# The last 64 tokens of v: from GpSimd's queue to SyncE's, and the first weights one per unit

## The chip, the cores and the metric

The kernel runs on one core of one Trainium2 chip. Five engines work side by side, each with its own queue of instructions in order: TensorE (PE; its weight loads are PEld), VectorE (DVE), ScalarE (ACT), GpSimd (POOL) and SyncE (SP). SP computes nothing and issues transfers. Sixteen transfer engines move data between memory and the core. The metric is the time of one execution on the device in microseconds, as the median of several runs; lower is better.

## The reference

There are two stages. The first is attention over a window of 128 tokens with a bias by distance, for 8 batches, 8 heads, 576 tokens and 64 numbers per head. The second takes attention's output as x (8 batches, 576 tokens, 512 channels), transforms it along the tokens, multiplies each of the 64 lowest modes by a complex matrix of its own, transforms back and mixes channels.

```
scores = q @ k.T / sqrt(64) - slope[h] * (i - j)      where 0 <= i - j < 128, else -1e9
x      = softmax(scores) @ v                          # heads side by side: (8, 576, 512)
X      = rfft(x over tokens)
Y[m]   = X[m] @ (w_r[m] + 1j * w_i[m])                for the modes m < 64, else 0
u      = x + irfft(Y)
out    = u + max(u @ w_ch, 0)
```

The two weights w_r and w_i hold 64 x 512 x 512 numbers each, 134 MB together, out of 164 MB that the kernel reads.

## The kernel before, in words

**Units and slots.** A unit is one pair of heads `s` of one batch `b`: 32 units (`g.units`, L69). The order comes from `GROUPS = ((0,), (1, 2, 3))` (L19): units 0 to 7 are pair 0 of the batches 0 to 7, and then come pairs 1, 2, 3 of batch 0, of batch 1, and so on. Attention runs in slots (`_slot`, L589), one for each unit, software-pipelined: in slot n come the scores of unit n (`_score`), the transposes of q and k of unit n+1 (`_tr`, evacuated by ACT in `_evac`), POOL's casts to bf16 of q and k of unit n+2 (`_cast_qk`) and of v of unit n+1 (`_cast_v`), and the product with v of unit n-1 (`_av`). The transposes take the PSUM buffers tagged `tqk`, of which there are two. The order of instructions on each engine is the order in which the program writes them; each engine waits at its next instruction until its inputs are there.

**Modes.** Pair 0's channels (rows 0 to 127 of each weight matrix) are multiplied between the slots from slot 10 on, two modes at a time (`_pair_of_modes`, `_modes`); the other 384 rows follow when attention is done. Weights come into a ring of 12,288 float32 per partition (`g.ring`). A part is two modes of w_r or of w_i: 512 KB for pair 0's rows, 1,536 KB for the other rows. The ring holds twelve of the small parts or four of the large. `_load_w` (L645) issues the next part if its place is free and does nothing if not; after each product with a part, `_modes` calls it as long as it succeeds. The steps from 16 modes on of the last group, the inverse transform and the mixing fill the rest of the time beside the weights, and `_finish` (L848) writes the output behind the last part.

**Transfers on SP's queue.** Loads ahead of the first slot are written in one loop (L126 to 134) over the units 0 to 15: q and k of the unit (`_load_unit`, one transfer each of 128 rows of 2,304 bytes, 288 KB), v of a unit (`_load_v`, two transfers of 128 KB in rows of 512 bytes; only the first 512 tokens), and from unit 7 on two calls of `_load_w`. As the ring has room for twelve small parts, the calls of units 7 to 12 take effect. v runs behind: v of unit n for n up to 4, and v of unit n-3 from unit 8 on. There are buffers for nine units of q and k (`QK`) and six of v (`VB`), so later loads wait for POOL's casts to free one. From slot 8 on each slot issues one more unit.

**The last 64 tokens of v.** The 576 tokens are four blocks of 128 and one of 64. v of the last 64 tokens has a tile of its own, `g.vbt`, in bf16: token p of the head `hh` of pair `s` on partition 64 `hh` + p, for each pair and batch, with a column of ones. `_load_vt` (L378) loads one pair `s` for all 8 batches: two transfers on POOL's queue, 128 KB each, in rows of 256 bytes (one token of one head). `_cast_vt` (L388) casts the pair with one POOL instruction of 128x512. Pair 0's load stands between the casts of units 0 and 1, ahead of the first slot, and its cast right behind the cast of v of unit 0 (L138 to 143). Pairs 1 to 3 are loaded in slots 2, 3 and 4 and cast in slots 4, 5 and 6 (L613 to 619). The one reader is the last pair of products in `_av` (L499), for every unit.

Of the kernel before, what the change touches and what calls it, by code (L numbers as in the profile page):

```python
# [9 lines left out]
FP32 = mybir.dt.float32  # L10
BF16 = mybir.dt.bfloat16
# [5 lines left out]
P = 128  # L17
MB = 8
GROUPS = ((0,), (1, 2, 3))  # L19
LA = 8  # L20
RING = 12288
JOINT = (2, 2)
ROWS = (2, 6)
VB = 6
# [12 lines left out]
LAST = (0, 3, 5, 6)  # L37

# [6 lines left out]
def kernel(  # L45
# [10 lines left out]
    nc = tc.nc  # L56
    B, H, S, D = q.shape
    NM, DM, _ = moe_w_r.shape
# [3 lines left out]
    g = Ctx()  # L62
# [27 lines left out]
    for b in range(B):  # L90
        t = [(g.x_sb[:, b, st], ((b, st * P), (b, st * P + 64))) for st in range(4)]
        if b % 2:
            t.append((g.x4[:, b // 2], ((b - 1, 4 * P), (b, 4 * P))))
        if b == B - 1:
            t = [t[4], t[1], t[0], t[3], t[2]]
        g.seq += t

    with tc.manual_schedule(engines={ET.SP, ET.PE, ET.Activation, ET.DVE, ET.Pool}):
        with ExitStack() as wctx:
# [5 lines left out]
            with ExitStack() as actx:  # L105
                cp = actx.enter_context(tc.tile_pool(name="const", bufs=1))
# [9 lines left out]
                g.vts = actx.enter_context(tc.tile_pool(name="vts", bufs=2))  # L116
# [9 lines left out]
                for n in range(n0):  # L126
                    _load_unit(g, n)
                    if n < VB - 1:
                        _load_v(g, n)
                    elif n >= VB + 2:  # L130
                        _load_v(g, n - 3)
                    if n >= g.first[1] - 1:
                        for _ in range(4 // JOINT[0]):
                            _load_w(g)
                with tc.tile_pool(name="tmpc", bufs=1, side="right") as tp:
                    _consts(g, tp)
                    _cast_qk(g, 0)
                    for s in GROUPS[0]:  # L138
                        _load_vt(g, s)
                    _cast_qk(g, 1)  # L140
                    _cast_v(g, 0)
                    for s in GROUPS[0]:
                        _cast_vt(g, s)
# [99 lines left out]
def _consts(g, tp):  # L243
# [15 lines left out]
    nc.gpsimd.memset(g.vbt[:, :, :, g.D : g.D + 1], 1.0)  # L259

# [117 lines left out]
def _load_vt(g, s):  # L378

    vt = g.vts.tile([P, g.B, g.D], FP32, tag="vt", name=f"vt{s}")  # L380
    for hh in range(2):
        g.nc.gpsimd.dma_start(
            out=vt[64 * hh : 64 * hh + 64],
            in_=g.v[:, 2 * s + hh, 512:576, :].rearrange("b p d -> p b d"))
    g.unit["vt", s] = vt


def _cast_vt(g, s):  # L388
    g.nc.gpsimd.tensor_copy(g.vbt[:, s, :, 0 : g.D], g.unit.pop(("vt", s)))
# [199 lines left out]
def _slot(g, n, w0, w1):  # L589
# [3 lines left out]
    if n == g.first[1] + 2:  # L593
        _select(g, 0, 0)
    if n < N:
        _score(g, n, 0)
# [16 lines left out]
    for j, grp in enumerate(GROUPS[1:]):  # L613
        for i, s in enumerate(grp):
            if n == g.first[j + 1] - 4 + i:
                _cast_vt(g, s)
        for i, s in enumerate(grp):
            if n == g.first[j + 1] - 6 + i:
                _load_vt(g, s)
# [300 lines left out]
```

## Time and profile before

| what | value |
|---|---|
| median of 3 runs | 449.3 us (448.2 to 451.52) |
| profiled execution, its own time | 450.29 us |
| its span | 448.5 us |
| busy PE / DVE / ACT / POOL | 294.1 / 216.1 / 189.6 / 139.1 us |
| bytes moved, mean rate | 173.86 MB, 388 GB/s |
| mean PE clock granted | 0.769 |
| POOL, casts of v (L409) | 128 of 64x256, 505 ns each |
| POOL, casts of q and k (L397) | 64 of 128x576, 768 and 859 ns each |
| POOL, issue of the tails (L382) | 8, 704 ns each, landing 7.5 us later (median) |
| POOL, casts of the tails (L389) | 4 of 128x512, 644 ns each; a wait of 4.5 us before the first |
| weights of pair 0's rows, issue to landing | 7.4 and 8.0 us (median of 32 and 33) |
| weights of the other rows, issue to landing | 13.8 and 13.7 us |

The span runs from the first to the last instruction of the profiled execution; the time holds a little more around it. A busy share is an average over stages with different limits: up to about 166 us there is attention with pair 0's modes between, up to 414 us the products with the other weights, and then the end. In the lists, L382 is line 382 of the kernel, `vt<-in_v_dram` means that the tile vt is written from the input v, and x8 that there were eight such instructions. In the chain of waits each line gives the start, the length and what the kernel waited for.

### The profile page before, as it was taken

To read this page: it belongs to the slowest core of one execution; us is meant where nothing else is said; L and a number is where in the kernel's file an instruction comes from. 1 tells how busy PE (TensorE), PEld (TensorE's weight loads), DVE (VectorE), ACT (ScalarE), POOL (GpSimd) and SP (SyncE) were. 2 spreads that over 40 slices of the span, in tenths; PEclk is the share of its full clock that TensorE was granted. 3 is DMA by queue.
4 is the path that set the end of the run, shared out by engine and by line. 5 is a ranking of instruction groups with operands and counts; after the bars stand their busy time and mean duration, and the time that the engine had idled before them with its cause. 6 is when DMAs were issued, how large, how long until landed. Compare 5 with 4: busy or idle time off the path is not lost.

```text
span 448.5 us, 12893 instructions
## 1 busy us (share of the span) xinstructions
PE 294.1 (66%) x5506; PEld 204.2 (46%) x5527; DVE 216.1 (48%) x427; ACT 189.6 (42%) x302; POOL 139.1 (31%) x257
## 2 busy tenths in 40 slices
PE   2467989887787885222235664854856748696993
PEld 2455767666666763111123333432433334464661
DVE  8458566566765661010002543453535345462882
ACT  3787656584866741000011331322313233251794
POOL 7699889586876702020000000000000000000700
PEclk9969576686988975555555988589778587899997
DMA  8999999999999999999999999999999999996498
GB/s 249 346 335 327 388 325 353 347 390 379 392 368 375 393 415 429 432 425 426 430 427 433 426 429 429 427 430 426 430 429 430 426 429 430 427 428 282 185 374 288
DMA packets 51562, 173.86 MB, mean 388 GB/s; under 512 B 4912, under 2 KB 21296, under 8 KB 43440
## 3 DMA queue, kind: packets, MB, share of 16 engines
q1 hardware_dynamic: 51120, 171.99, 97.2%
q0 software_dynamic: 384, 1.05, 0.9%
q8 instruction: 43, 0.70, 0.6%
q14 instruction: 15, 0.12, 0.1%
HBM read 163.58 MB, written 9.44 MB: 386 GB/s over the span
## 4 chain that ended last, share of the span: by engine, by line
DMA 50%; PE 26%; ACT 10%; DVE 6%; issue 4%; POOL 2%; ACTq 0%; POOLq 0%
DMA ring<-in_moe_w_r_dram 47%; ACT att L459 6%; PE acc L704 5%; PE sc L447 4%; PE xt L539 4%; PE u L825 3%; PE av L493 3%; DMA ring<-in_moe_w_i_dram 3%; ACT qkT L428 3%; PE tqk L420 2%; PE u L745 2%; POOL qkb L397 1%; PE xw L758 1%; DVE x_sb L507 1%; ACT mask L311 1%
## 5 line engine op out<-in xcount | busy, mean ns | idle before, releaser
L704 PE MATMUL acc<-Xz,ring 128*128 128x32 bf16 x2048 | 70.7, 183 | 100.2 <-DMA ring<-in_moe_w_r_dram 51.0
L704 PEld LDWEIGHTS <-ring 128*128 128x128 bf16 x2048 | 61.3, 101 | 130.1 <-DMA ring<-in_moe_w_r_dram 65.1
L763 ACT CAST hl<-xw 64x512 bf16<-64x512 f32 x72 | 41.7, 579 | 105.6 <-PE xw L758 70.9
L459 ACT ACTIVATE att<-sc 128x1024 bf16<-128x1024 f32 x64 | 65.6, 1025 | 32.8 <-PE sc L447 26.7
L764 DVE TENSOR_TENSOR hl<-xw,hl 64x512 bf16<-64x512 f32 x72 | 49.6, 688 | 58.1 <-ACT hl L763 57.8
L409 POOL CAST vb<-v 64x256 bf16<-64x256 f32 x128 | 64.7, 505 | 20.1 <-PE av L493 13.7
L783 POOL MEMSET ZTa<- 32x512 bf16 x2 | 1.0, 515 | 187.5 <-ACT ZTa L781 187.5
L447 PE MATMUL sc<-qkT,qkT 64*64 64x256 bf16 (+1 forms) x512 | 32.4, 330 | 30.1 <-ACT qkT L428 16.3
L758 PE MATMUL xw<-wch,xT 128*128 128x512 bf16 x138 | 46.3, 467 | 2.7 <-issue 2.2
L428 ACT COPY qkT<-tqk 128x576 bf16<-128x576 bf16 x64 | 40.7, 638 | 0.6 <-PE tqk L420 0.6
L420 PE MATMUL tqk<-ident_b,qkb 64*64 64x64 bf16 x1152 | 31.7, 214 | 7.6 <-POOL qkb L397 6.9
L420 PEld LDWEIGHTS <-qkb 64*64 64x64 bf16 x1152 | 30.8, 130 | 10.2 <-POOL qkb L397 9.2
L464 DVE TENSOR_TENSOR att<-att,mask 128x1024 bf16<-128x1024 bf16 x32 | 26.9, 839 | 14.7 <-ACT att L459 14.5
L585 ACT ACTIVATE Xz<-xz 128x192 bf16<-128x192 f32 (+1 forms) x24 | 7.5, 313 | 59.0 <-DVE Xz L584 57.9
L493 PE MATMUL av<-vb,att 128*128 128x65 bf16 (+1 forms) x512 | 30.8, 215 | 0.6 <-issue 0.2
L584 DVE CAST Xz<-xz 128x384 bf16<-128x384 f32 (+1 forms) x24 | 12.0, 511 | 36.4 <-PE xz L578 35.7
L447 PEld LDWEIGHTS <-qkT 64*64 64x64 bf16 x512 | 13.1, 120 | 35.3 <-ACT qkT L428 18.8
L397 POOL CAST qkb<-k 128x576 bf16<-128x576 f32 x32 | 27.5, 859 | 0.0
L493 PEld LDWEIGHTS <-att 128*128 128x128 bf16 (+1 forms) x512 | 24.4, 111 | 6.5 <-issue 0.6
L397 POOL CAST qkb<-q 128x576 bf16<-128x576 f32 x32 | 24.6, 768 | 6.1 <-PE tqk L420 3.3
L738 DVE COPY xT<-tp 128x512 bf16<-128x512 bf16 x36 | 15.2, 421 | 21.9 <-PE tp L736 21.4
L469 DVE TENSOR_TENSOR att<-att,mask 128x1024 bf16<-128x1024 bf16 x32 | 25.0, 780 | 1.5 <-ACT att L459 1.1
(104 smaller groups left out, 395.2 us busy)
## 6 DMA issues: line engine op xcount, KB each, us to landing
ring<-in_moe_w_r_dram SPq DMA_DIRECT2D x32, 1536.0 KB, 13.8
ring<-in_moe_w_i_dram SPq DMA_DIRECT2D x31, 1536.0 KB, 13.7
ring<-in_moe_w_i_dram SPq DMA_DIRECT2D x33, 512.0 KB, 8.0
ring<-in_moe_w_r_dram SPq DMA_DIRECT2D x32, 512.0 KB, 7.4
q<-in_q_dram SPq DMA_DIRECT2D x32, 288.0 KB, 6.3
k<-in_k_dram SPq DMA_DIRECT2D x32, 288.0 KB, 6.2
v<-in_v_dram SPq DMA_DIRECT2D x64, 128.0 KB, 5.8
out_dram<-o SPq DMA_DIRECT2D x32, 256.0 KB, 3.3
```

The costliest lines, as they stand in the source:

```text
L397: g.nc.gpsimd.tensor_copy(tb, t)
L409: g.nc.gpsimd.tensor_copy(o[64 * r : 64 * r + 64, i], v[64 * i : 64 * i + 64, r])
L420: g.nc.tensor.transpose(tp[hs, r, :], u.b[w][hs, r], g.ident_b[hs, hs], tile_position=(64 * hh, 64 * hh))
L428: g.nc.scalar.copy(dst.rearrange("c (p r) -> c p r", r=g.R), u.tp[w].rearrange("c r p -> c p r"))
L447: nc.tensor.matmul(sc[64 * r : 64 * r + 64, hh, 256 * i : 256 * i + nq], lhsT=kT[hs, c * P + r : c * P + P : 2], rhs=qT[hs, c * P : c * P ...
L459: nc.scalar.activation(a, sc, AF.Exp, scale=1.0 / math.sqrt(g.D))
L464: nc.vector.tensor_tensor(out=a, in0=a, in1=m, op=ALU.mult)
L493: nc.tensor.matmul(av[o, hh, col(t)], lhsT=att[c // 2][:, hh, q0 : q0 + m], rhs=u.vb[:, 2 * c + hh, 0 : D + 1], start=(j == 0), stop=(t < ...
L704: nc.tensor.matmul(acc[:, et, :, m0 - c0 : m0 - c0 + n, :], lhsT=wt[:, a, et * P : (et + 1) * P], rhs=X[:, a, 1 - w : 3 - w, m0 % MB : m0 ...
L758: nc.tensor.matmul(xw, lhsT=xT[:, dt], rhs=g.wch[:, dt], start=(dt == 0 and n in RELU), stop=(dt == 3))
L763: nc.scalar.copy(g.hl[own, n, h], xw[own])
L764: nc.vector.tensor_tensor(out=g.hl[other, n, h], in0=xw[own], in1=g.hl[own, n, h], op=ALU.subtract)
```

## The change

The tails of v are loaded by batch in place of by pair, on SP's queue in place of POOL's, and in rows of 512 bytes (two neighbouring tokens of one head) in place of 256. One batch is two transfers of 64 KB, each with four heads: 32 rows per head, laid on partitions as they come, so that partition 4p + h holds the tokens 2p and 2p+1 of head h of the four. Batch i of 0 to 7 is issued with unit 4, 5, 6, 7, 9, 10, 11 and 12 (`VT`), behind that unit's q, k and v. From unit 4 on each unit calls `_load_w` once, so that the twelve parts are spread over the units 4 to 15.

POOL casts a batch's tails as they lie, in one instruction of 128x256, first thing in slot b+1. Then PE puts the tokens on their partitions: four products with matrices of zeros and ones (`g.selv`, made at the start by POOL with one memset and four copies of the identity), 128x128 each with 128 columns, into a PSUM tile that shares the tag `tqk` with the transposes. DVE copies the result, 128x256, into `g.vbt`. The products stand behind slot b+1's scores and casts and ahead of the spectrum and `_av`. The tiles for the loaded tails have six buffers in place of two. The column of ones and everything that reads `g.vbt` are as before.

```diff
+VT = (4, 5, 6, 7, 9, 10, 11, 12)
...
-                g.vts = actx.enter_context(tc.tile_pool(name="vts", bufs=2))
+                g.vts = actx.enter_context(tc.tile_pool(name="vts", bufs=VB))
+                g.selv = cp.tile([P, 2, 2, P], BF16, name="selv")
...
-                    if n >= g.first[1] - 1:
-                        for _ in range(4 // JOINT[0]):
-                            _load_w(g)
+                    if n in VT:
+                        _load_vt(g, VT.index(n))
+                    if n >= VT[0]:
+                        _load_w(g)
...
-                    for s in GROUPS[0]:
-                        _load_vt(g, s)
                     _cast_qk(g, 1)
                     _cast_v(g, 0)
-                    for s in GROUPS[0]:
-                        _cast_vt(g, s)
...
+    nc.gpsimd.memset(g.selv, 0.0)
+    src = g.ident_b.rearrange("p (m i h) -> p i h m", i=2, h=2)
+    for r in range(2):
+        for i in range(2):
+            nc.gpsimd.tensor_copy(
+                g.selv[:, i, r].rearrange("p (h m r) -> p r h m", h=2, r=2)[:, r], src[:, i])
...
-def _load_vt(g, s):
-    vt = g.vts.tile([P, g.B, g.D], FP32, tag="vt", name=f"vt{s}")
-    for hh in range(2):
-        g.nc.gpsimd.dma_start(
-            out=vt[64 * hh : 64 * hh + 64],
-            in_=g.v[:, 2 * s + hh, 512:576, :].rearrange("b p d -> p b d"))
-    g.unit["vt", s] = vt
-def _cast_vt(g, s):
-    g.nc.gpsimd.tensor_copy(g.vbt[:, s, :, 0 : g.D], g.unit.pop(("vt", s)))
+def _load_vt(g, b):
+    vt = g.vts.tile([P, 2, 2, g.D], FP32, tag="vt", name=f"vt{b}")
+    for i in range(2):
+        g.nc.sync.dma_start(
+            out=vt[:, i].rearrange("p r d -> p (r d)"),
+            in_=g.v[b, 4 * i : 4 * i + 4, 512:576].rearrange("h (p r) d -> p h (r d)", r=2))
+    g.unit["vt", b] = vt
+def _cast_vt(g, b):
+    t = g.work.tile([P, 2, 2, g.D], BF16, tag="vtb", name="vtb")
+    g.nc.gpsimd.tensor_copy(t, g.unit["vt", b])
+    g.unit["vt", b] = t
+def _put_vt(g, b):
+    t = g.unit.pop(("vt", b))
+    ps = g.ps1.tile([P, 2, 2, g.D], FP32, tag="tqk", name="pvt")
+    for i in range(2):
+        for r in range(2):
+            g.nc.tensor.matmul(
+                ps[:, :, i], lhsT=g.selv[:, i, r], rhs=t[:, :, r], start=(r == 0), stop=(r == 1))
+    g.nc.vector.tensor_copy(
+        g.vbt[:, :, b, 0 : g.D], ps.rearrange("p j i d -> p (j i) d"))
...
+    if 0 <= n - 1 < g.B:
+        _cast_vt(g, n - 1)
     if n < N:
         _score(g, n, 0)
...
-    for j, grp in enumerate(GROUPS[1:]):
-        for i, s in enumerate(grp):
-            if n == g.first[j + 1] - 4 + i:
-                _cast_vt(g, s)
-        for i, s in enumerate(grp):
-            if n == g.first[j + 1] - 6 + i:
-                _load_vt(g, s)
+    if 0 <= n - 1 < g.B:
+        _put_vt(g, n - 1)
     if 0 <= n - 2 < N - 1:
         _spectrum(g, n - 2)
     if 0 <= n - 1 < N:
         _av(g, n - 1)
```

## The prediction

> **What bounds the kernel now.** I read the chain of waits first, then the page's transfer rows, then the stretches of time around the loads that the change moves, and last the waits of the engines that it touches.
>
> The chain of waits is made of compute alone up to 166 us and of weight transfers after that:
>
> ```profile
> 164.23 0.70 DVE att L469
> 164.98 0.82 PE av L493 x9
> 166.35 11.95 DMA ring<-in_moe_w_r_dram
> 178.35 0.84 PE acc L704 x24
> 179.20 13.68 DMA ring<-in_moe_w_r_dram
> ```
>
> From that alone, attention's compute would seem to bound the first 166 us. The transfer rows say that it does not bound alone:
>
> ```profile
> DMA  8999999999999999999999999999999999996498
> GB/s 249 346 335 327 388 325 353 347 390 379 392 368 375 393 415 429 432 425 426 430 427 433 426 429 429 427 430 426 430 429 430 426 429 430 427 428 282 185 374 288
> ...
> q0 software_dynamic: 384, 1.05, 0.9%
> ```
>
> The transfer engines are busy in every slice until the weights end, and only the bytes per second differ. So whatever takes transfer time early pushes the whole queue of weights, whose last part arrives at 414.17 us (issued at 401.60, 12.57 us in the chain); the stretch behind it is the same work. A smaller transfer bill is worth its own size at the end, as long as compute frees the buffers in time. The ring of weights shows that it does: SP issues part 12 at 67.16 us, though PE had used part 0, whose place it takes, by 58.9 us: 8 us in hand. Only from about 160 us does SP issue within a microsecond of PE's release, and there eight parts of 512 KB, about 10 us of transfer, are in flight.
>
> What do the tails of v (row q0, 1.05 MB, issued by POOL at L382) cost in that bill? These stretches show it (columns: stretch, its length, POOL busy, PE clock, share of the transfer engines, GB/s):
>
> ```profile
> core 0: us, POOL busy (x), PEclk, DMA share, GB/s
> 10.00:13.00 3.00, 0.01 (x1) 1.00 1.10 224
> 18.00:20.00 2.00, 1.89 (x4) 1.00 1.05 391
> 20.00:30.00 10.00, 9.59 (x17) 0.83 1.03 389
> 30.00:33.00 3.00, 2.87 (x6) 0.50 1.07 203
> 36.00:38.00 2.00, 1.64 (x4) 1.00 1.03 240
> 42.00:44.00 2.00, 1.94 (x4) 0.93 0.99 245
> 56.00:60.00 4.00, 2.54 (x5) 1.00 1.05 348
> 60.00:66.00 6.00, 5.70 (x11) 0.57 0.96 305
> 84.00:88.00 4.00, 0.49 (x1) 0.50 0.93 292
> 152.00:165.00 13.00, 3.32 (x6) 0.93 1.03 416
> ```
>
> Four times the engines are as busy as ever and move a little over half as much: 10 to 13, 30 to 33, 36 to 38 and 42 to 44 us. Each follows a pair of POOL's issues (5.56, 26.25, 30.99, 36.98 us), which land 7.5 us later.
>
> **The change, part by part, and its sum.** The sum is against the profiled execution, 450.29 us (span 448.5 and 1.8 around it). The median of the runs shown is 449.3, 1.0 lower; I take the difference found here off that median.
>
> *Old tails go.* The four stretches last 10 us and move 224x3 + 203x3 + 240x2 + 245x2 = 2,251 KB. With the 1,049 KB of tails taken out, 1,202 KB of other loads remain, which at 370 GB/s (between 348 and 389 in the rows beside them) need 3.2 us. The tails cost 10 - 3.2 = 6.8 us. Lower end: the packets' own time, 0.9% of 448.5 = 4.0 us. Upper end 7.5: some tail packets fall just outside the stretches. I take 6.8, since the loss of rate is seen directly.
>
> *New tails come.* 16 transfers of 64 KB in 512-byte rows. The nearest row is v itself, also 512-byte rows on SP's queue. Units without weights (590 KB of q and k, 262 KB of v) go at 348 GB/s in 56 to 60 us: 2.45 us each. The q and k alone go at 391 (18 to 20 us): 1.51 us. That leaves 0.94 us for 262 KB, so 3.8 us for all tails. By the 305 GB/s of 60 to 66 us it is 5.1 us. I take 4.2, nearer the first, because in 60 to 66 us the engines' share itself drops under 1. Transfer sum: -6.8 + 4.2 = -2.6; ends -7.5 + 3.8 = -3.7 and -4.0 + 5.1 = +1.1. The Trainium skill (DMA: Bandwidth & Descriptors, Specifications) says that rows reach line rate from 512 bytes on, and shorter ones are read and written back; at the 416 GB/s of the 4 KB rows the new tails would cost 2.5 us and the sum would be -4.3. The trace does not agree: v's 512-byte rows go at 262 KB in 0.94 us, 279 GB/s.
>
> *Weights one per unit from unit 4 to 15, not two per unit from 7 to 12.* The same twelve parts, the same bytes. Units 13 to 15 no longer go without weights, so half of the low stretch 60 to 66 us may fill: 6 x (1 - 305/348) = 0.74, half is 0.4. Against it: a transfer's issue waits for the arrival of the one eight issues before (the records carry eight semaphores in turn), and small transfers put fewer bytes in flight: seven per 1.51 MB in units 9 to 12, so 1.7 MB, as in 60 to 66 us. Ends: -0.74, and 4 units x (1.51 MB/305 - 1.51 MB/348) = +2.4. I take -0.4. Landing times are 5.8 us for 128 KB and 6.3 for 288 KB, so a small one holds its place as long as a large one, which the +2.4 covers. The Trainium skill (the same page, Bandwidth) calls transfers under 64 KB descriptor-dominated, and the new ones lie at that edge.
>
> *Units and v moved later.* q and k of units 5 to 8 and v 5 on stand behind more. Counting bytes, v5 comes after 9.5 MB; the kernel before has moved 9.6 MB by 30 us, and v5's cast stands at 34.3: 4 us cover. Part 11, issued last, is wanted at about 83 us: 20 us cover. Gone, each microsecond would delay the slot by as much.
>
> *SP.* Sixteen issues of 0.38 us, 6 us in all. In 30 to 50 us SP waits 10 us for arrivals, so they fit; without that cover every later load would slip by 0.8 us per batch.
>
> *POOL.* Off: eight issues (5.6 us), four casts (2.6) and the one wait of 4.5 us at 10 us. On: eight casts of 128x256, about 0.33 each by half of L389's 0.61 (2.6), and at the start a memset and four copies (0.5 by L783, 4 x 0.27 between L336's 0.20 and L255's 0.30: 1.6 us). POOL idles 0.99 there, so the first cast is 0.6 late; ACT waits 2.57 us for the mask at 12 us, which hides it. PE waits for POOL's casts 1.9 us in 38 to 46 us; that goes.
>
> *PE and DVE.* Per batch, in slots 1 to 8: four products 128x128 (L539's shape, 0.27 each: 1.06 us, or 0.6 overlapped as the x4 groups are) and one copy 128x256 out of PSUM (L584's same shape: 0.41). Over eight batches 5 to 8.5 us on PE and 3.3 on DVE. DVE waits 11.4 us for av in 5 to 60 us and hides its share; PE wins 1.9 and loses about 5, so attention's front may be 3 us later. Cover: the 8 us that the ring has in hand, shrinking to the 10 us of transfers in flight at 166 us. I cost it at 0; gone, it costs what the slip exceeds.
>
> *The new wait.* The cast of a tail now stands at the top of POOL's slot, ahead of q, k and v, and the products ahead of av on PE. POOL reaches these slots at 19.2, 23.0, 27.7, 32.4, 38.3, 42.8, 47.2 and 51.7 us. By bytes (4.4 MB for batch 0, 11.0 for batch 4, 15.5 for batch 7; moved before by 16, 35 and 48.5 us, less what the old tails cost and plus the new till then) tails are in by about 17, 34 and 46 us: 2 to 5 us cover, 0 cost. Gone, all that stands behind in the slot waits: q, k and v on POOL, av on PE.
>
> Sum: -2.6 - 0.4 = -3.0: profiled 447.3, median **446.3**.
>
> **Rivals.**
> 1. *More than that:* the old tails at 7.5, the new at 3.8, the low stretches 60 to 66 (0.74) and 84 to 88 us (4 x (1 - 292/386) = 1.0) both filled, because POOL's and DMA's lead carries on. -3.7 - 0.74 - 1.0 = -5.4: 443.9. A variant: 512-byte rows cost no more per byte than 4 KB rows in this place, -4.3 - 0.4, 444.6; it gets a quarter of this rival's chance, v's own rate being against it. That is the line-rate rule of the Trainium skill named above. For the rival: SP waits on arrivals more than on PE till 150 us. Against: in 84 to 88 us PE is at half clock.
> 2. *The change doesn't bring what it says:* 512-byte rows from four heads, one per partition, cost as much as the old ones. +1.1 at most with -0.4: 449 to 450. For it: the packets' own 0.9%. Against: the four dips.
> 3. *Slower:* the products in PE's in-order queue. If all eight slots pay 1.06 + 0.41 = 1.47 us, 11.8 less 1.9 is a slip of 9.9 us. At 166 us part 64 is issued on PE's release, and part 63 before it lands at 174.5 by its 9.9 us; with transfers 3 us ahead, slip beyond about 3 us leaves the queue empty. 446.3 + 6.9 = 453.2, and 455.1 if POOL's relief wins nothing; it decides from 3 us on. For it: PE is 4.9 of 5 us busy in 45 to 50 at half clock. Against: PE waits for ACT and POOL in most slots up to 44 us.
>
> **How the numbers follow.** Forecast 0.58 (its own range 444.5 to 448), more 0.22, no gain 0.10, slower 0.10. The runs shown spread 0.4% either side, so about 1% (4.5 us) is what this kernel can tell from no change. Faster than that, under 444.8: rival 1 and 0.05 of the forecast, 0.27. Slower, over 453.8: most of rival 3, 0.07. Same: 0.66. Range 442.8 to 450.8: it takes in rivals 1 and 2 and leaves out rival 3 and a far end.
>
> **What would show it.** Right: no row q0 of 1 MB; GB/s of 350 or more through 30 to 44 us; the last part's issue near 398.5 us instead of 401.6; no long waits of POOL for vt or PE for the cast. Wrong: rates of 300 in 27 to 47 us (the places in flight); POOL waiting for vt; part 64 issued later than 166 us with the engines idle before it.

## The result, and the profile after

| | kernel before | changed kernel |
|---|---|---|
| median, same chip, 21 runs each | 448.4 us (446.03 to 451.52) | 450.07 us (447.71 to 454.17) |
| profiled span, its PE clock | 448.5 us, 0.769 | 450.4 us, 0.767 |

The ratio after to before is 1.0043, with a 95% interval from 1.0024 to 1.0063: slower by about 1.9 us, where 3.0 us less was forecast. Forecast and measurement are 5 us apart. The two profiled executions took 450.3 and 452.2 us, each about 2 us more than its kernel's median.

The bytes are as announced. On the page of the changed kernel, the row q0 is gone, and these are the transfer engines' share by slice, their rate, and the one queue that is left:

```profile
DMA  8998999999999999999999999999999999996598
GB/s 268 331 353 277 326 360 330 351 372 392 383 382 389 410 417 419 430 424 426 431 429 425 431 428 428 429 426 431 428 428 429 426 429 429 426 428 276 196 333 313
...
q1 hardware_dynamic: 53424, 173.04, 97.4%
```

Beside the slices shown of the kernel before, the first and third rose (249 to 268, 335 to 353 GB/s), and the fourth and fifth fell (327 to 277, 388 to 326): the loss moved, it didn't go. Shorter stretches say where. The columns are those of the table in the prediction:

```profile
10.00:13.00 3.00, 2.85 (x6) 1.00 1.09 357
18.00:20.00 2.00, 1.96 (x5) 1.00 0.78 264
30.00:33.00 3.00, 2.57 (x4) 0.66 1.03 339
36.00:38.00 2.00, 0.26 (x1) 1.00 0.90 333
38.00:42.00 4.00, 3.32 (x8) 0.61 0.69 176
42.00:44.00 2.00, 2.00 (x3) 0.94 0.96 321
```

The four dips of the old tails are filled (224, 203, 240, 245 before; 357, 339, 333, 321 now). In their place stand two of another kind. In the old dips the engines were fully busy with costly packets. In 18 to 20 and 38 to 42 us their share is 0.78 and 0.69, where a full stretch shows 1.0 to 1.1: too little had been issued for them in time.

The wait that the prediction costed at nothing is the longest of POOL between 5 and 60 us (total, times, longest):

```profile
POOL vtb L395 <- DMA vt<-in_v_dram: 10.1, 5, 3.2
...
POOL vb L428 <- DMA v<-in_v_dram: 0.4, 1, 0.4
```

The chain of waits still turns from compute to transfers at part 64 (the ring's issues on SP, counted from 0). That point has moved from 166.35 to 171.13 us:

```profile
169.01 0.70 DVE att L488
169.76 0.81 PE av L512 x9
170.77 0.36 PE acc L720 x10
171.13 8.27 DMA ring<-in_moe_w_r_dram
...
180.30 14.13 DMA ring<-in_moe_w_r_dram
```

Compute is 4.8 us later there, and the end of the profiled execution only 1.9. Most of the 4.8 doesn't arise where the tails are waited for. POOL's cast of q shows how far attention has come: for unit 10 it starts at 51.7 us before and at 52.9 after, for unit 15 at 71.6 and 72.0, and only for unit 19 at 89.9 and 93.1. In the changed kernel without its sixteen loads (an experiment below) it starts at 46.0, 65.9 and 85.6, so the loads do hold attention, but up to unit 15 about as much as the old ones did. What costs the 3 us between units 15 and 19 isn't shown, nor whether every execution has it.

Why the end isn't 4.8 us later is read from SP's issues of the weights (start, length). First the kernel before, parts 63, 64, 66 and 67, then the changed one, the same parts:

```profile
164.54 0.53 SPq L661 DMA_DIRECT2D ring<-in_moe_w_i_dram  x1
166.35 0.53 SPq L661 DMA_DIRECT2D ring<-in_moe_w_r_dram  x1
...
171.21 0.54 SPq L661 DMA_DIRECT2D ring<-in_moe_w_r_dram  x1
174.93 0.54 SPq L661 DMA_DIRECT2D ring<-in_moe_w_i_dram  x1
```

```profile
168.43 0.70 SPq L677 DMA_DIRECT2D ring<-in_moe_w_i_dram  x1
171.13 0.54 SPq L677 DMA_DIRECT2D ring<-in_moe_w_r_dram  x1
...
175.65 0.54 SPq L677 DMA_DIRECT2D ring<-in_moe_w_r_dram  x1
176.35 0.59 SPq L677 DMA_DIRECT2D ring<-in_moe_w_i_dram  x1
```

Part 67 takes the last place of the ring that pair 0's weights held. Two things must have happened: part 63, the last of pair 0's, has landed and is used (0.5 us after its landing), and compute has come that far. How long compute takes is read from a run in which part 63 had long landed (166.07 us, without the old tails): 5.2 us from part 64's issue (162.40) to part 67's (167.62). Before, part 63 landed at 174.45, so the transfers decided (174.9), and compute, which would have been ready at 166.35 + 5.2 = 171.6, had 3.4 us in hand. After, part 63 landed at 175.62 (176.1) and compute was ready at 171.13 + 5.2 = 176.3: compute decided, by 0.2 us. The later of the two gives the issue of part 67 within 0.2 us in 18 of the 19 profiles in the table below (with two issues of 1 MB it comes 0.6 us earlier). From part 67 to the end it is 273 to 275 us in 17 of them (276 and 280 in the others), mostly transfers. So in these two executions **both** bounds are later after the change: transfers by 1.2 us, compute by 4.8.

### The profile page after: what moved, and what is told of

Its sections match the earlier page's. It is cut to its first block, busy times and chain, and to the rows that moved or that the text cites. A ratio compares the mean times of both kernels' runs of the same rounds, so it can differ in the third digit from the quotient of the medians.

```text
span 450.4 us, 12961 instructions
## 1 busy us (share of the span) xinstructions
PE 298.4 (66%) x5538; PEld 209.9 (47%) x5559; DVE 217.4 (48%) x435; ACT 190.0 (42%) x302; POOL 136.2 (30%) x258
## 4 chain that ended last, share of the span: by engine, by line
DMA 54%; PE 24%; ACT 6%; DVE 6%; SPq 3%; issue 3%; POOL 1%; ACTq 0%; POOLq 0%
DMA ring<-in_moe_w_r_dram 43%; DMA k<-in_k_dram 5%; PE acc L720 4%; ACT att L478 4%; PE xt L558 3%; PE sc L466 3%; PE u L841 3%; PE av L512 3%; DMA ring<-in_moe_w_i_dram 3%; DMA vt<-in_v_dram 2%; PE u L761 1%; PE tqk L439 1%; DMA v<-in_v_dram 1%; PE xw L774 1%; ACT qkT L447 1%
## 5 line engine op out<-in xcount | busy, mean ns | idle before, releaser
L720 PE MATMUL acc<-Xz,ring 128*128 128x32 bf16 x2048 | 69.9, 183 | 98.0 <-DMA ring<-in_moe_w_r_dram 48.4
L720 PEld LDWEIGHTS <-ring 128*128 128x128 bf16 x2048 | 61.3, 101 | 127.1 <-DMA ring<-in_moe_w_r_dram 63.0
L428 POOL CAST vb<-v 64x256 bf16<-64x256 f32 x128 | 59.3, 463 | 23.4 <-PE av L512 18.7
L774 PE MATMUL xw<-wch,xT 128*128 128x512 bf16 x138 | 47.7, 479 | 2.6 <-issue 2.0
L439 PEld LDWEIGHTS <-qkb 64*64 64x64 bf16 x1152 | 32.5, 135 | 8.2 <-POOL qkb L416 6.2
L483 DVE TENSOR_TENSOR att<-att,mask 128x1024 bf16<-128x1024 bf16 x32 | 27.1, 848 | 12.9 <-ACT att L478 12.9
L512 PE MATMUL av<-vb,att 128*128 128x65 bf16 (+1 forms) x512 | 32.0, 219 | 1.5 <-DVE att L488 0.9
L416 POOL CAST qkb<-q 128x576 bf16<-128x576 f32 x32 | 27.4, 858 | 5.3 <-PE tqk L439 3.0
L512 PEld LDWEIGHTS <-att 128*128 128x128 bf16 (+1 forms) x512 | 25.5, 114 | 7.5 <-DVE att L488 1.3
L774 PEld LDWEIGHTS <-xT 128*128 128x128 bf16 x144 | 17.2, 120 | 19.6 <-issue 12.6
L466 PEld LDWEIGHTS <-qkT 64*64 64x64 bf16 x512 | 13.3, 122 | 27.1 <-ACT qkT L447 14.3
```

What stands on the lines that cost most here:

```text
L416: g.nc.gpsimd.tensor_copy(tb, t)
L428: g.nc.gpsimd.tensor_copy(o[64 * r : 64 * r + 64, i], v[64 * i : 64 * i + 64, r])
L439: g.nc.tensor.transpose(tp[hs, r, :], u.b[w][hs, r], g.ident_b[hs, hs], tile_position=(64 * hh, 64 * hh))
L466: nc.tensor.matmul(sc[64 * r : 64 * r + 64, hh, 256 * i : 256 * i + nq], lhsT=kT[hs, c * P + r : c * P + P : 2], rhs=qT[hs, c * P : c * P ...
L483: nc.vector.tensor_tensor(out=a, in0=a, in1=m, op=ALU.mult)
L512: nc.tensor.matmul(av[o, hh, col(t)], lhsT=att[c // 2][:, hh, q0 : q0 + m], rhs=u.vb[:, 2 * c + hh, 0 : D + 1], start=(j == 0), stop=(t < ...
```

## The experiments

Theory at the start: the sixteen issues on SP and the tails that land just in time make the loss (it is called F or S below, by what is at stake: F, attention's front held by POOL's wait; P, by POOL's own time; S, SP's issues). The rivals: the prediction's own view that only the transfer bill counts (T); the products on PE; the order of the weights. The granted clock is none: its mean over the changed kernel's 21 executions is 0.783, as it is over the 18 of the kernel before beside the first experiments. In the table, the ratio is to the kernel before on the same chip, and the issues of the parts 12, 64 and 67 (us) and the column "decided by" are of one profiled execution each, while executions of one kernel spread over 5 us or more (446.0 to 451.5 before); so a difference of 2 us between two issues shows nothing by itself, and the ratio decides. (The run with early tails and the cast on DVE has no issues here: its profiled execution took 459.8 us, its median is 452.6.)

| run | ratio, 95% interval | part 12 | part 64 | part 67 | decided by |
|---|---|---|---|---|---|
| before | 1 | 67.2 | 166.4 | 174.9 | transfers |
| changed | 1.0043 (1.0024 to 1.0063) | 70.2 | 171.1 | 176.4 | compute |
| weights' order alone | 1.0007 (0.9979 to 1.0036) | 65.5 | 163.6 | 171.2 | transfers |
| tails alone | 1.0077 (1.0048 to 1.0106) | 69.9 | 167.8 | 175.2 | transfers |
| no old tails | 0.9903 (0.9871 to 0.9934) | 59.2 | 162.4 | 167.6 | compute |
| no new loads | 0.991 (0.9878 to 0.9943) | 59.5 | 163.3 | 168.5 | compute |
| one load per batch | 1.0064 (1.004 to 1.0088) | 70.3 | 170.7 | 175.7 | compute |
| new loads by POOL | 1.005 (1.0025 to 1.0074) | 63.0 | 168.1 | 173.3 | compute |
| loads of 8 KB | 0.9998 (0.9968 to 1.0029) | 67.5 | 169.2 | 174.4 | compute |
| old rows on SP | 1.0011 (0.9991 to 1.0031) | 70.9 | 167.2 | 175.1 | transfers |
| cast behind q, k, v | 1.0114 (1.0067 to 1.0162) | 67.7 | 169.8 | 175.0 | compute |
| early tails | 1.0055 (1.0028 to 1.0083) | 69.7 | 165.5 | 173.8 | transfers |
| both of these | 1.0114 (1.0077 to 1.0151) | 69.1 | 172.9 | 178.2 | compute |
| early tails, DVE cast | 1.0085 (1.0056 to 1.0115) | | | | |
| no loads, POOL's casts x4 | 1.009 (1.0055 to 1.0125) | 64.1 | 169.2 | 174.4 | compute |
| no loads, DVE copies | 1.001 (0.9989 to 1.0032) | 61.3 | 167.9 | 173.1 | compute |
| before, cast in slot 1 | 0.9994 (0.9974 to 1.0015) | 66.8 | 165.6 | 173.3 | transfers |
| the same, weights' order | 1.0021 (0.9995 to 1.0047) | 68.9 | 165.6 | 173.7 | transfers |
| sixteen issues, 8 KB | 0.9993 (0.9962 to 1.0024) | 66.6 | 162.3 | 171.7 | transfers |
| two issues, 1 MB | 0.9923 (0.9892 to 0.9955) | 61.9 | 163.1 | 167.7 | compute |

**The parts, one at a time.** The weights' order alone, in the kernel before:

```diff
-                    if n >= g.first[1] - 1:
-                        for _ in range(4 // JOINT[0]):
-                            _load_w(g)
+                    if n >= 4:
+                        _load_w(g)
```

> The kernel before with only the weights moved: one part per unit from unit 4 to 15; the tails of v stay on POOL's queue. Theory 'thin queue' (the sixteen small transfers on SP's queue take issue time and places, so the transfer engines run short of work, and that eats the gain from the old tails): the spread of the weights by itself costs nothing, -1 to +0.5 us against before. Rival 'weights first' (q, k and v of units 5 to 8 stand behind weights that nobody needs yet, and attention starts late): +1.5 to +3 us, with POOL waiting for q, k or v before 45 us. Rival 'late front' (POOL's 10.1 us of waits for tails and the products push attention back): no tails moved, so 0.

The tails alone, the changed kernel with the two lines of the old order back:

> The changed kernel with the weights as before: two parts per unit from unit 7 on; the tails by SP as in the change. Theory 'thin queue': the tails alone make the loss, +1 to +2.5 us against before, and in the stretch of units 9 to 12 two parts per unit put more bytes behind each tail, so it may be a little better than the changed kernel. Rival 'weights first': the loss goes, and the forecast gain of 2.6 us comes, -2 to -3 us. Rival 'late front': with two parts per unit the tails of batches 4 to 7 arrive still later than in the changed kernel, so +3 us or more.

The kernel before without its tail transfers, POOL filling the tails with zeros:

```diff
-    vt = g.vts.tile([P, g.B, g.D], FP32, tag="vt", name=f"vt{s}")
...
-    g.nc.gpsimd.tensor_copy(g.vbt[:, s, :, 0 : g.D], g.unit.pop(("vt", s)))
+    g.nc.gpsimd.memset(g.vbt[:, s, :, 0 : g.D], 0.0)
```

> The kernel before without the eight transfers of the tails of v: POOL writes zeros into their places where the casts stood, so the output of the last 64 tokens lacks v. It measures what the old tails cost in all. The prediction's 6.8 us: -6 to -7.5 us against before. Rival 'cheap tails' (only the packets' own time): -4 us or less. If attention's front were the bound instead of transfers: -2 to -3 us, since POOL wins back 5.6 us of issues of which PE waited 1.9.

And the changed kernel without its sixteen transfers, all casts, products and copies left in:

```diff
-    vt = g.vts.tile([P, 2, 2, g.D], FP32, tag="vt", name=f"vt{b}")
...
-    g.unit["vt", b] = vt
+    if b == 0:
+        g.vt0 = g.vts.tile([P, 2, 2, g.D], FP32, tag="vt", name="vt0")
+    g.unit["vt", b] = g.vt0
```

> The changed kernel without its sixteen transfers of tails: POOL casts a tile of zeros instead, and the products, the copies and the weights' order stay, so the output of the last 64 tokens lacks v. Theory 'thin queue': all of the loss goes with the transfers, -6 to -7.5 us against before, as in the run without the old tails. Rival 'products' (32 products, 8 copies and 8 casts push attention back): it stays 3 us or more behind the run without the old tails. Rival 'late front' by waiting for tails: as 'thin queue' here, since nothing is waited for; the stretches of GB/s tell them apart in the other runs.

The weights' order does nothing alone; with the tails on SP it is worth 1.5 us (1.0077 against 1.0043, the intervals overlap). The tails alone lose 3.5 us, more than the 1 to 2.5 that the first theory gave them. The old tails cost (1 - 0.9903) x 448.4 = 4.4 us, the new loads (1.0043 - 0.991) x 448.4 = 6.0. The two kernels without transfers are alike (0.9903 and 0.991, a difference known to about 2 us), so selection products, copies and casts as such cost nothing that can be measured: the rival of the products on PE, at 3 us or more, falls. The loss is the loads' on both sides of the sum.

**The form of the loads.** One transfer of 128 KB per batch in rows of 1,024 bytes:

```diff
-    for i in range(2):
...
+    g.nc.sync.dma_start(
+        out=vt.rearrange("p i r d -> p (i r d)"),
+        in_=g.v[b, :, 512:576].rearrange("h (p r) d -> h p (r d)", r=4))
```

> The changed kernel with one transfer of 128 KB per batch in rows of 1,024 bytes in place of two of 64 KB in rows of 512; the products are left as they are, so the last 64 tokens of v land in wrong places. So far the run without the new transfers is 1.3% (6.0 us) faster than the changed kernel, where bytes at the rate of v's rows account for 3.8. Theory 'places and issues' (each small transfer takes one of eight places in flight and 0.55 us of SP): half of them gone gives back about half of what is over, and more if the queue then never runs dry: 1.5 to 3 us faster than the changed kernel, -1.5 to +0.5 against before. Rival 'scattered rows' (rows from eight heads cost what they cost): about 1 us from the longer rows, so +1 against before. Rival 'late front': as 'places and issues', with POOL's waits for tails gone.

The same sixteen transfers on POOL's queue, batches 0 and 1 ahead of the first slot, batch n+2 in slot n:

```diff
-        g.nc.sync.dma_start(
+        g.nc.gpsimd.dma_start(
...
+    if 2 <= n + 2 < g.B:
+        _load_vt(g, n + 2)
```

> The changed kernel with the same sixteen transfers in 512-byte rows issued by POOL (batches 0 and 1 ahead of the first slot, batch n+2 in slot n), so they take no place and no time of SP's queue; POOL pays 16 x 0.7 = 11 us for issues. Theory 'places and issues': the loss on SP goes, and rows of 512 cost less than the old rows of 256, which cost 4.4 us in all: -1 to -2.5 us against before, unless POOL's 11 us of issues make attention late. Rival 'scattered rows': no better than the changed kernel, +2. Rival 'POOL pays' (casts wait behind the issues): +2 us or more, with PE waiting for POOL's casts.

Sixteen transfers on SP of 8 KB each, an eighth of the bytes, that POOL still waits for:

```diff
-            out=vt[:, i].rearrange("p r d -> p (r d)"),
-            in_=g.v[b, 4 * i : 4 * i + 4, 512:576].rearrange("h (p r) d -> p h (r d)", r=2))
+            out=vt[0:16, i].rearrange("p r d -> p (r d)"),
+            in_=g.v[b, 4 * i, 512:544].rearrange("(p r) d -> p (r d)", r=2))
```

> The changed kernel with its sixteen transfers cut to 16 rows of 512 bytes each (8 KB in place of 64 KB, one head of four, so most of the last 64 tokens of v is zero; POOL clears the cast tile each time). It measures places and issues almost without bytes. The run without the transfers stands at -4.0 us against before. Theory 'places and issues': most of the cost stays, -2 to 0 us against before, with SP issuing late as in the changed kernel. Rival 'scattered rows' (it is the bytes in these rows): the cost goes, -3.5 to -4 us.

The old 256-byte rows by pair, but on SP with the units 4, 6, 8 and 10, weights one per unit, pair 0's cast in slot 1:

```diff
+                    if n in (4, 6, 8, 10):
+                        _load_vt(g, (4, 6, 8, 10).index(n))
...
-        g.nc.gpsimd.dma_start(
+        g.nc.sync.dma_start(
```

> The kernel before with its old transfers (by pair, 256-byte rows, eight of 128 KB) issued by SP with units 4, 6, 8 and 10, the weights one per unit from unit 4, and pair 0's cast in slot 1; no products. It takes eight places in place of sixteen, with rows half as long. Theory 'places and issues': better than the changed kernel, -1 to +1 us against before, if short rows cost on SP's queue no more than on POOL's. Rival 'rows' (256-byte rows are the cost whoever issues them, 512-byte rows half of it): +1 to +4 us against before.

On POOL's queue the same bytes in the same rows let part 12 go at 63.0 us, 7.2 us earlier than from SP's: rows of 512 bytes aren't the cost. The Trainium skill says in DMA: Bandwidth & Descriptors, Rules for kernel authors, that issuing from another engine wins no bandwidth and "only saves sequencer issue time"; part 12 agrees. But POOL pays for it, 16 issues of 0.55 us, and the time is no better: a transfer lead of 4.2 us at part 12 over the kernel before isn't seen in the ratio (1.005; in the profiled execution part 67 goes 1.6 us earlier than in the one before, so single profiles don't rank two kernels this close). An eighth of the bytes brings part 12 forward only by 2.7 us; its ratio, 0.9998, keeps about 4 of the 6.0 us. The old rows on SP, eight issues, are the same as the kernel before (1.0011), as the theory of issues had it, and not 1 to 4 us slower, as the rival had it; but their part 12 goes as late as with sixteen (70.9).

One transfer per batch missed what S would have it do. With eight issues SP waited again (14.7 us between 12 and 50 us, against 7.5 in the changed kernel), yet POOL waited 11.1 us for vt, the transfer engines moved only 342 and 317 GB/s in 20 to 30 and 40 to 50 us at shares of 1.04 and 1.05, and the time was no better. So fewer issues alone don't help in this form. The form changed more than the number of issues, though. The trace has sixteen arrival marks, one per transfer engine, for each of the changed kernel's transfers of the tails whose landing it tells; for each of these eight it has nine, one 1.1 us after the issue and eight at the end. If that means eight engines in place of sixteen, each with twice the bytes of a batch, it fits the landings, 4.7 to 8.2 us after the issue (3.3 to 6.4 in the changed kernel), and so POOL's waits. This run is then no clean test of the number of issues; why the full engines move less there isn't settled.

**Where the wait stands.** POOL's cast moved behind its casts of q, k and v:

```diff
-    if 0 <= n - 1 < g.B:
-        _cast_vt(g, n - 1)
     if n < N:
         _score(g, n, 0)
...
     if 0 <= n - 1 < g.B:
+        _cast_vt(g, n - 1)
         _put_vt(g, n - 1)
```

> The changed kernel with each batch's cast of the tails moved on POOL from the top of slot b+1 to behind that slot's casts of q, k and v, just ahead of the products. The transfers are the same. Theory F (POOL's in-order wait for tails that land just in time pushes attention's front back, and the front sets when part 67 is issued): the casts of q, k and v are not held any more, POOL's wait for vt shrinks from 10.1 us to under 5, part 64 is issued 2 to 4 us earlier than 171.1, and the time falls by 1.5 to 4 us, to a ratio of 0.995 to 1.001 against the kernel before. Theory T (the transfer engines' lost time between 13 and 50 us is what costs): the same transfers in the same order, so the ratio stays at 1.002 to 1.006.

Batch b with unit b+2:

```diff
-VT = (4, 5, 6, 7, 9, 10, 11, 12)
+VT = (2, 3, 4, 5, 6, 7, 8, 9)
```

> The changed kernel with batch b's tails issued with unit b+2 (2 to 9 in place of 4 to 7 and 9 to 12), so that they land some 3 to 8 us ahead of their cast; q, k and v of the units behind them come that much later. Theory F: POOL's wait for vt falls under 3 us, but what it waits for may become q, k and v; if the tails alone were late, part 64 at 168 us or earlier and a ratio of 0.996 to 1.001. Theory T: as many transfers with as many bytes on the same queue, ratio 1.002 to 1.006, with POOL's wait moved from vt to q, k and v.

Both:

> Both: the tails issued with unit b+2, and their cast behind the casts of q, k and v. Theory F: no wait for vt of any size, part 64 at 165 to 168 us, ratio 0.994 to 1.0. Theory T: 1.002 to 1.006.

And early tails, cast by DVE (`nc.vector` in place of `nc.gpsimd`) ahead of the products:

> The changed kernel with the tails issued with unit b+2 and cast by DVE just ahead of the products, so that POOL neither casts nor waits for them. Theory P: POOL gains 10 us of waits and 5 us of casts, less what v then lets it wait (7.8 us in 3 waits with early tails): part 64 at 163 to 168 us, ratio 0.994 to 1.0. Theory T, or the loop of any engine: the loads land as late as before and DVE or PE waits in POOL's place, ratio 1.003 to 1.01.

F missed the time of all four. POOL's wait for vt went to nothing in the first, but POOL then waited 4.8 us for v, PE still 5.3 us for the cast (6.3 in the changed kernel), and the ratio came out higher; its profiled execution, the fastest of its six, doesn't show why. With early tails POOL waited 7.8 us for v; compute was early enough (part 64 at 165.5), and then the transfers decided (173.8), at 1.0055. So moving the wait doesn't help: q, k, v and tails together land as late as they are needed, and a wait taken from one is met at the next. Why the two with the cast behind q, k and v are slower than the changed kernel isn't shown.

**Are there two bounds?** Four runs take one side away and load the other. No loads, and POOL's casts done four times, then no loads and four more DVE copies per batch:

```diff
-    g.nc.gpsimd.tensor_copy(t, g.unit["vt", b])
+    for _ in range(4):
+        g.nc.gpsimd.tensor_copy(t, g.unit["vt", b])
```

> The changed kernel without its sixteen transfers (the casts read a tile of zeros, so the tails' share of the output is left out), and with each batch's cast done four times in place of once: some 1.2 us more for POOL at the top of each of the slots 1 to 8, 10 us in all, about as long as POOL waits for vt in the changed kernel. Transfers run as without the tails: part 12 at about 59.5 us. Theory F: attention's front slips, part 64 is issued 3 to 6 us later than the 163.3 us without the repeats, and the time grows by 2 to 5 us, from a ratio of 0.991 to 0.996 to 1.002, though no transfer was added. Theory T: POOL's time is hidden, ratio 0.988 to 0.994.

```diff
+    for _ in range(4):
+        o = g.work.tile([P, 2, 2, g.D], BF16, tag="scr", name="scr")
+        g.nc.vector.tensor_copy(o, g.vt0)
```

> The changed kernel without its sixteen transfers (the tails' share of the output is left out), with one cast per batch, and four more copies of 128x256 by DVE behind each batch's copy: some 1.2 us more for DVE in each of the slots 1 to 8, 8 to 10 us in all, where the run on POOL had as much there. Theory P: DVE idles a third of that time and the copies mostly fit beside POOL's chain, so the ratio stays at 0.989 to 0.997. The rival, that attention is a tight loop in which any engine's time counts: 1.003 to 1.01, as with POOL.

The kernel before with pair 0's cast, and its wait of 4.5 us, moved from ahead of the first slot into slot 1, and that with the weights' new order:

```diff
-                    for s in GROUPS[0]:
-                        _cast_vt(g, s)
...
+    if n == 1:
+        _cast_vt(g, 0)
     if 0 <= n - 1 < N:
         _av(g, n - 1)
```

> The kernel before with one line moved: POOL's cast of pair 0's tails, which waits 4.5 us for them at 10 us, goes from ahead of the first slot to the end of POOL's work in slot 1, still ahead of its first reader. The same transfers from the same queues. Theory P (POOL's chain of casts sets attention's pace in the slots 0 to 9, and a wait in it goes to the end at nearly its own size): the wait is gone or under 1 us, unit 4's cast of q stands at 19 to 20 us in place of 23.0, part 64 is issued 2 to 4 us earlier than 166.35, and the time falls by 1.5 to 4 us, ratio 0.991 to 0.997. Theory T (the time that the tails take from the transfer engines is what costs): nothing changes there, ratio 0.998 to 1.002.

> The same with the first weights one part per unit from unit 4 on. Theory P: as the run before or up to 1 us better, ratio 0.989 to 0.997, since with an earlier front the transfers bind at part 67 and the spread of the weights may help them. Theory T: 0.998 to 1.002, as the weights' order alone gave 1.0007.

Compute alone makes it slower. Without any tail transfer, POOL's extra casts (24 of 0.40 us or more, at least 9.6 us) took the ratio from 0.991 to 1.009, or 8 us (part 67 goes 5.9 us later), and DVE's 32 copies (0.50 us each, some 16 us) to 1.001, 4.5 us. POOL's time is the dearer, but the second run fell between the range of P and that of its rival: DVE's time isn't free either in the slots 1 to 8. In the run with POOL's casts, part 63 landed at 171.72, so transfers would have let part 67 go at 172.2; it waited for compute (part 64's issue, then part 67's):

```profile
169.20 0.54 SPq L676 DMA_DIRECT2D ring<-in_moe_w_r_dram  x1
...
174.43 0.54 SPq L676 DMA_DIRECT2D ring<-in_moe_w_i_dram  x1
```

Relief of compute alone gives nothing, against P, with the weights' order as before (0.9994) or new (1.0021). The wait of 4.5 us is gone in the kernel before with the late cast, and unit 4's cast of q stands at 18.9 in place of 23.0 us; but at 47 us the lead is down to 0.9, since POOL now waits for v:

```profile
POOL vb L407 <- DMA v<-in_v_dram: 5.9, 5, 1.9
```

Part 12 goes where it went (66.8), and the time is the same. The runs without tails, which relieve both sides, are the ones that gain.

**Issues or bytes?** The kernel without loads gets sixteen transfers of 8 KB in the places of the tails, or two of 512 KB with the units 4 and 9; no instruction waits for either:

```diff
+    for i in range(2):
+        g.nc.sync.dma_start(
+            out=vt[0:16, i].rearrange("p r d -> p (r d)"),
+            in_=g.v[b, 4 * i, 512:544].rearrange("(p r) d -> p (r d)", r=2))
```

> The changed kernel with its casts reading a tile of zeros (the tails' share of the output is left out), and sixteen transfers of 8 KB in the places of the changed kernel's, into a tile that nobody reads. No engine waits for them; an eighth of the bytes is moved. Theory S (the new tails cost SP's issues, 16 of about 0.5 us in stretches where SP has no wait left to hide them): part 12 at 64 to 68 us in place of 59.5, and as transfers and compute stand within 1.3 us of each other at part 67 without tails, most of it reaches the end: ratio 0.996 to 1.002. The rival, the bytes: part 12 at 59.5 to 61, ratio 0.989 to 0.994.

```diff
+    if b in (0, 4):
+        vt = g.vts.tile([P, 16, g.D], FP32, tag="vt", name=f"vt{b}", bufs=1)
+        g.nc.sync.dma_start(
+            out=vt.rearrange("p r d -> p (r d)"),
+            in_=g.v.rearrange("b h n d -> (b h n) d")[0:2048].rearrange("(p r) d -> p (r d)", r=16))
```

> The same with two transfers of 512 KB in rows of 4 KB (1 MB, as the tails have) on SP's queue with the units 4 and 9, into a tile that nobody reads. Theory S: two issues of 0.6 us and the bytes' own time, 1.05 MB at 390 GB/s or 2.7 us: part 12 at 61 to 63 us, ratio 0.990 to 0.996. The rival, the bytes: part 12 at 64 to 70, ratio 0.997 to 1.004.

Both came as S said. The issues alone take the ratio from 0.991 to 0.9993, 3.7 us, though they move 0.13 MB; 1 MB in two issues takes it to 0.9923, 0.6 us and within the interval. Part 12 moves by 7.1 us for the issues and by 2.4 for the bytes. And the stretches of the run with the issues alone show the idle engines of the changed kernel, with next to no bytes added:

```profile
18.00:20.00 2.00, 1.85 (x5) 1.00 0.84 252
...
38.00:42.00 4.00, 3.14 (x7) 1.00 0.92 307
```

Without the issues the same stretches have a share of 1.02 each, at 400 and 368 GB/s. One thing the run doesn't part: an issue takes SP's time and also one of the eight places that SP's queue has in these programs (each issue waits for the arrival of the one eight before it), for the 4.5 us that even 8 KB need to land (median).

## Why the prediction was wrong, point by point

**The step that failed: "Sixteen issues of 0.38 us, 6 us in all. In 30 to 50 us SP waits 10 us for arrivals, so they fit".** The reading of 10 us was right (10.9), the rest is off. An issue of these transfers took 0.60 us (median, the least 0.55), 10.3 us in all sixteen. And SP's waits don't lie where the first issues stand: four of the eight batches go out between 12 and 24 us, where SP had waited 3.4 us in all. SP's queue in the kernel before, and then in the changed one (start, length):

```profile
14.59 0.34 SPq L362 DMA_DIRECT2D q<-in_q_dram  x1
15.22 0.34 SPq L362 DMA_DIRECT2D k<-in_k_dram  x1
```

```profile
14.94 1.54 SPq L367 DMA_DIRECT2D k<-in_k_dram  x1
16.52 1.20 SPq L387 DMA_DIRECT2D vt<-in_v_dram  x2
17.77 0.61 SPq L677 DMA_DIRECT2D ring<-in_moe_w_i_dram  x1
18.42 0.59 SPq L367 DMA_DIRECT2D q<-in_q_dram  x1
19.06 0.43 SPq L367 DMA_DIRECT2D k<-in_k_dram  x1
19.53 1.19 SPq L387 DMA_DIRECT2D vt<-in_v_dram  x2
```

Before, SP waits for a place ahead of most issues up to 16.8 us and again from 24.2 us on; between them it too issues without a gap. After, one issue stands right behind the other from 13 to 26 us, and each starts when the one ahead of it ends, not when a place comes free (at 18.42 the place had been free since 16.32). Between 12 and 50 us SP spent 21.0 us on 39 issues before, 30.5 us on 52 after, and the transfer engines ran dry beside it. Single issues of 1.4 to 1.5 us, like k's at 14.94, stand in both kernels (before: 1.39 at 16.83); here one lies close ahead of the first idle stretch and one at the start of the second (38.09, 1.37). Ahead of the second there was a wait as well:

```profile
34.22 0.35 SPq L367 DMA_DIRECT2D k<-in_k_dram  x1
36.57 0.89 SPq L378 DMA_DIRECT2D v<-in_v_dram  x2
37.50 1.96 SPq L387 DMA_DIRECT2D vt<-in_v_dram  x2
```

SP stood for 2.0 us (34.57 to 36.57) until the k issued eight transfers before had landed (36.50), and then needed 2.9 us to issue 384 KB. Some of the eight places were held by transfers of 64 KB. So in 13 to 26 us SP's time is what limits, in 30 to 50 us its time and the places together. In the kernel before a load of q takes SP as a rule 0.34 or 0.35 us where it had waited and up to 0.59 right behind another issue; the 0.38 of the working is what v takes (median).

**Old tails, -6.8.** At the transfers' side they were worth 8.0 us (part 12 at 59.2 without them, 67.2 with), so the reading of the four dips was sound. At the end they are worth 4.4, in its range of -7.5 to -4.0; compute decides next (part 67 at 167.6).

**New tails, +4.2.** At part 12 they cost 10.7 (59.5 to 70.2), at the end 6.0. The bytes as such are the small part: 2.4 at part 12 for as many bytes in two issues, 3.5 for the same rows by POOL's queue, near the 3.8 to 5.1 of the working. The term holds for a transfer whose issue costs nothing; what it lacked is the issues. The working's own price for SP without cover, 0.8 us per batch or 6.4 in all, is close to what the loads cost at the end.

**Weights, -0.4.** +0.3 with an interval of -0.9 to +1.6, which holds the -0.4. That run has no small transfers on SP, so it doesn't test the far end of +2.4, "the places in flight"; the wait of 2.0 us above is a sign of them.

**PE and DVE, 0.** Right, but not by the cover named. The products cost 218 ns each (median), the copies 425, and without the loads they leave no trace in the time. With the loads PE waits 6.3 us ahead of them for POOL's casts.

**The new wait, "2 to 5 us cover, 0 cost".** POOL waited 10.1 us, ahead of five of the eight casts. Two things were off. The cover was counted from the times at which POOL reached these slots in the kernel before (19.2, 38.3 and 51.7 us for batches 0, 4 and 7), though the working itself takes issues and a wait of 4.5 us off POOL ahead of them; POOL came at 14.3, 34.6 and 50.6. And the later tails were late: batch 0 landed at 17.2 us (said: 17), batch 4 at 37.6 (said: 34) and batch 7 at 52.5 (said: 46). So the wait of 3.1 us for batch 0 is POOL's being early, the 2.0 for batch 7 the landing's slip, and the 3.2 for batch 4 some of each. Beside the changed kernel without loads, attention is 6.9 us later at unit 10 (52.9 against 46.0) and 7.8 at part 64; beside the kernel before, which had its own wait, 1.2 at unit 10. Moving the wait doesn't help, since v is as late.

**The premise, "A smaller transfer bill is worth its own size at the end, as long as compute frees the buffers in time", with "8 us in hand".** The condition failed. The 8 us belong to part 12; at part 67, where it is decided, compute had 3.4 us in hand in the profiled execution. The 8 us of the old tails ended as 4.4, and the 4.2 us lead of POOL's queue as nothing. The third rival's "it decides from 3 us on" was right (3.4), its cause, the products' own time, wrong. What would show the prediction wrong did show: POOL waiting for vt, part 64 later than 166 us, rates under 300 (176 GB/s in 38 to 42 us).

What stays open: how the changed kernel's 6.0 us divide. The issues alone make 3.7 (SP's time and the places together) and the bytes about 0.6; the remaining 1.7 fits the waits of compute for the late tails, but that is a difference of separate runs, as wide as their intervals, and wasn't isolated. Open too are the 3 us of the profiled execution between units 15 and 19. No version beat both kernels; the nearest, the late cast in the kernel before, is the same as it (0.9994).

## What to carry to other kernels

Before an edit is costed at nothing because its engine waits elsewhere, ask whether it waits in the very stretch where the edit stands; a queue that only issues transfers has a rate of its own, here 0.4 to 0.6 us per transfer back to back, and a transfer of 64 KB spends as much of it as one of 512 KB. Where compute and transfers both run just in time, find the instruction at which they meet and write down what each has in hand there: a gain on one side counts up to that margin, a loss on the other from it on.

## What the runs showed that was not expected

SP's time for an issue isn't set by the size: 0.42 us for 8 KB, 0.60 for 64 KB and 0.60 for 512 KB (medians of the sixteen 8 KB and 64 KB transfers and of the weights between 12 and 50 us), and 0.43 for the 288 KB of k right behind another issue. The Trainium skill says of small transfers in DMA: Bandwidth & Descriptors, Rules for kernel authors, "under 64 KB you're paying mostly overhead". The runs with 8 KB agree, and what is paid there is SP's time and its places, not the transfer engines' time: sixteen of them cost 3.7 us, 1 MB in two transfers 0.6.

POOL's time in attention's slots is worth some 0.6 to 0.8 us at the end for each microsecond (5.9 at part 67, 8 in the time, for 9.6 or a little more), DVE's in the same slots some 0.3 (4.5 for 16).
